# Spectra of a long convolution: one 1024-wide product, sums in PSUM, 64-row halves, and an order written out as a table

## The chip, the cores and the metric

The kernel runs on one core of a Trainium2 chip. The metric is device time in microseconds (us), the median of three runs. A core has five engines that run side by side, each with its own queue in program order: TensorE for matmuls (PE in the profile; PEld is its weight load), VectorE (DVE), ScalarE (ACT), GpSimd (POOL) and SyncE (SP), which here issues the DMAs. Matmuls write to PSUM, in banks of 512 fp32 values for each of 128 partitions. Everything else lies in SBUF.

## The reference

```python
mod = (_silu(c) @ w_mod).reshape(c.shape[0], 6, 1, -1)
h = _layernorm(x, axis=-1) * (1 + ca) + sa
x = x + ga * _A_ref(h, ...)          # the convolution
h = _layernorm(x, axis=-1) * (1 + cb) + sb
x = x + gb * _B_ref(h, ...)          # gated FFN: (silu(h@w1) * (h@w3)) @ w2
...
# in _A_ref: u is h, of length L = 2048 and 640 channels
P = jnp.exp((A * dt[:, None])[:, :, None] * pos[None, None, :])
K = 2.0 * jnp.einsum("dn,dnl->dl", C, P).real
Kf = jnp.fft.rfft(K, L2)             # L2 = 2 * L
Uf = jnp.fft.rfft(u_t, L2)
y = jnp.fft.irfft(Uf * Kf[None, :, :], L2)[:, :, :L]
```

For each of 640 channels a filter `K` of 2048 taps is made from 128 complex modes, the input is convolved with it through Fourier transforms, and the result goes through a layer norm and a gated FFN of width 1728.

## The kernel before

The channels go in five blocks of 128 (b = 0 to 4). For each block four kinds of work run:

- The filter is made in eight chunks of 16 channels (tasks `g`). POOL adds phases (`ph`, 1024 wide) and multiplies magnitudes (`yy`, `xx`, 512 wide, three for each chunk); ACT takes sines (`tr`, in PSUM); DVE multiplies (five instructions on `yy` and `xx`); PE forms the product `kps` in 32 matmuls of 64 columns, four abreast in 32-column groups; ACT copies it to `ks` and DVE adds the skip term (`ks<-kps,dsk`). `yy`, `xx` and `ph` have two buffers each.
- The input is normalised (tasks `h`: ACT or DVE makes `hn`, DVE makes `hb`), goes through a scratch tensor in DRAM and comes back turned (`xb`).
- A first stage of the transform turns `xb` and `ks` each into `sp` (or `sp2` for `xb` of odd blocks), in eight tasks (names `hh` and `k`): eight matmuls into one bank `ps`, then one copy by ACT or DVE.
- The spectra (tasks `w`, eight for each block): PE makes the second stage of both sides, `fh` and `fk`, in PSUM; ACT copies `fh` to `hz`; DVE multiplies the two complex spectra into `fp`. After each second one (tasks `z`, four for each block) PE takes the inverse of `fp` into two banks `fz`, ACT or DVE copies them to `zt`, and SP stores them to the DRAM scratch `zd`.

The complex product before takes four DVE instructions: with r for the real or imaginary half of the input's spectrum, two of 512 values, the second in place in the PSUM bank `fk`, and two of 256 values that take the difference and the sum:

```python
to = k if r else prod[i // 2][:, :, i % 2 * 2:i % 2 * 2 + 2, :].rearrange("p r q d -> p q r d")
nc.vector.tensor_mul(to, k, bc(held[i][:, :, r], 2, 2))
...
k = bank.pop((1, i))
for r, op in enumerate((ALU.subtract, ALU.add)):
    p = prod[i // 2][:, r, i % 2 * 2:i % 2 * 2 + 2, :]
    nc.vector.tensor_tensor(p, p, k[:, :, 1 - r], op=op)
```

When the last block's `zd` is stored, the memory is laid out anew ("border"), the inverse is finished (`iy`, `iyb`), the second layer norm runs, and the FFN follows: matmuls of 512 columns with each operand split into a high and a low part (`fp32r`), PE after PE, to the end. An fp32 matmul has two records in the profile, so a task of eight matmuls is x16 there.

All work up to the first groups of the FFN is entered as tasks in a class `Plan`: name, engine or choice of engines, an estimated duration, what it follows, and which ring buffers it takes and gives back. A ring of four PSUM banks (`bank`) serves `ps`, `fh`, `fk`, `fz`. `Plan.place` plays the tasks through by their estimated durations with a table of ranks (`RANKS`) as priorities, and this sets each engine's order and the choice of engine before anything runs. Each engine then follows that order strictly. All those instructions carry one line number (L157, the recording helper), so they are told apart by tile names.

## Time and profile before

| | us |
|---|---|
| runs: median of 3 (lowest, highest) | 974.97 (973.5, 975.03) |
| profiled execution, its time | 972.31 |
| profiled execution, span from first to last instruction | 970.5 |
| busy in the span: PE, DVE, ACT, POOL | 859.9, 702.0, 546.4, 340.5 |
| last filter product (`kps`) starts, in the span | 346.1 |
| last inverse (`fz`) starts | 374.6 |

A row of a group reads: line, engine, operation, output<-inputs, sizes (partitions x values), count | busy us, mean ns of one | idle time of the engine just before them, and what ended it. A row of the timeline reads: start, duration, engine, line, operation, and in brackets the idle time before it. Instructions of one engine overlap a little at their ends, so the distance from start to start is what one of them takes of the engine.

### The profile page before, as it was taken

How to read it: one execution, taken by the hardware profiler on the slowest of the kernel's cores; microseconds unless marked ns; L12 is line 12 of the kernel's file. 1: busy time of each engine (PE TensorE's matmuls, PEld its weight loads, DVE VectorE, ACT ScalarE, POOL GpSimd, SP SyncE). 2: the span in 40 equal slices, each digit the busy share in tenths (PEclk: the TensorE clock that was granted, in tenths of full speed). 3: DMA queues.
4: the chain of work that ended last, by engine and by line, in shares of the span. 5: the costliest groups of instructions: out<-in, count | busy, mean ns of one | idle time of the engine just before them, and what ended most of it. 6: DMA issues, size and time to landing. Idle time of an engine off the chain costs nothing.

```text
span 970.5 us, 20551 instructions
## 1 busy us (share of the span) xinstructions
PE 859.9 (89%) x7985; PEld 681.8 (70%) x7985; DVE 702.0 (72%) x1395; ACT 546.4 (56%) x1022; POOL 340.5 (35%) x371
## 2 busy tenths in 40 slices
PE   1464787889899997899999999999999999999997
PEld 1132665767778884677777778888788888888775
DVE  7998899999999968886767677557456464645422
ACT  6877788979888851564434455346444344443412
POOL 1797889879799600002111111000011212120000
PEclk9996999999999999799999999999999999999999
DMA  9955453723425268935434422276342322220374
GB/s 218 275 168 191 111 136 95 177 66 106 111 80 152 74 159 206 241 118 182 122 120 139 122 96 68 82 209 194 112 134 64 102 77 86 82 82 28 108 220 133
DMA packets 110506, 127.31 MB, mean 131 GB/s; under 512 B 10568, under 2 KB 90696, under 8 KB 109128
## 3 DMA queue, kind: packets, MB, share of 16 engines
q1 hardware_dynamic: 109032, 125.21, 45.3%
q8 instruction: 63, 1.03, 0.5%
q10 hardware_dynamic: 1376, 0.79, 0.3%
q14 instruction: 35, 0.29, 0.1%
HBM read 95.82 MB, written 30.15 MB: 130 GB/s over the span
## 4 chain that ended last, share of the span: by engine, by line
PE 70%; DVE 17%; ACT 5%; issue 4%; DMA 3%; POOL 1%; SPq 1%; ACTq 0%; DVEq 0%
PE c L157 19%; PE acc L157 18%; PE X L157 12%; PE ps L157 4%; PE gu L157 3%; DVE yy L157 3%; PE kps L157 3%; PE fz L157 2%; PE fk L157 2%; DVE fp L157 2%; PE fh L157 2%; DVE hn L157 2%; DVE xx L157 2%; DVE xb L157 1%; ACT tr L157 1%
## 5 line engine op out<-in xcount | busy, mean ns | idle before, releaser
L157 PE MATMUL acc<-ah,w 128*128 128x512 f32 x560 | 173.2, 395 | 2.4 <-DMA w<-w2d 1.7
L157 PEld LDWEIGHTS acc<-ah,w 128*128 128x128 f32 x560 | 103.7, 188 | 26.4 <-issue 2.1
L157 PE MATMUL acc<-al,w 128*128 128x512 f32 x260 | 102.4, 394 | 0.0
L665 DVE TENSOR_TENSOR wl<-s,wh 128x256 fp32r<-128x256 f32 x92 | 38.9, 423 | 67.5 <-ACT wh L664 67.1
L841 POOL TENSOR_TENSOR s<-wr 128x256 f32<-128x256 f32 x22 | 16.4, 744 | 187.8 <-DMA wr<-in_w 94.8
L157 POOL TENSOR_TENSOR ph<-p,p 128x1024 int32<-128x1024 int32 x40 | 79.2, 1979 | 8.2 <-ACT tr L157 8.0
L664 ACT ACTIVATE wh<-s 128x256 fp32r<-128x256 f32 x92 | 37.6, 410 | 78.5 <-PE X L157 58.1
L157 PE MATMUL kps<-yy,xx 128*32 128x64 f32 x2560 | 51.8, 234 | 28.6 <-DVE xx L157 21.4
L157 DVE TENSOR_TENSOR yy<-yy,tr 128x512 f32<-128x512 f32 (+1 forms) x80 | 75.3, 943 | 1.2 <-ACT tr L157 0.6
L157 PEld LDWEIGHTS kps<-yy,xx 128*32 128x32 f32 x2560 | 45.1, 116 | 38.3 <-issue 22.0
L664 ACT ACTIVATE wh<-wr 128x256 fp32r<-128x256 f32 x92 | 38.4, 418 | 56.0 <-PE X L157 42.3
L842 POOL TENSOR_TENSOR s<-s,wr 128x256 f32<-128x256 f32 x22 | 16.6, 755 | 134.0 <-issue 133.9
L902 ACT ACTIVATE t<-g 128x512 f32<-128x512 f32 x44 | 27.8, 632 | 52.7 <-DVE g L866 52.7
L157 ACT ACTIVATE tr<-ph,hpi 128x512 f32<-128x512 f32 x80 | 54.6, 690 | 4.4 <-DVE xx L157 2.7
L157 PEld LDWEIGHTS acc<-al,w 128*128 128x128 f32 x260 | 48.9, 188 | 10.8 <-DVE al L665 0.3
L871 DVE SCALAR_TENSOR_TENSOR g<-t,g 128x512 f32<-128x512 f32 x48 | 33.7, 702 | 31.3 <-ACT t L902 29.3
L157 POOL TENSOR_TENSOR yy<-e,e 128x512 f32<-128x512 f32 x48 | 52.4, 1109 | 8.8 <-PE kps L157 5.9
L157 DVE TENSOR_TENSOR xx<-tr,xx 128x512 f32<-128x512 f32 x80 | 54.3, 680 | 1.1 <-ACT tr L157 1.1
L157 PE MATMUL ps<-wk,ks 128*64 128x128 f32 x640 | 42.4, 285 | 13.6 <-DVE ks L157 8.9
L157 ACT ACTIVATE tr<-ph 128x512 f32<-128x512 int32 x80 | 47.3, 598 | 12.4 <-DVE yy L157 6.5
L157 PE MATMUL ps<-wk,xb 128*64 128x128 f32 x640 | 46.1, 295 | 6.3 <-ACT sp L157 3.0
L157 PEld LDWEIGHTS ps<-wk,ks 128*64 128x64 f32 x640 | 37.0, 143 | 20.3 <-ACT hn L157 6.6
(448 smaller groups left out, 2379.7 us busy)
## 6 DMA issues: line engine op xcount, KB each, us to landing
w<-w2d SPq DMA_DIRECT2D x42, 640.0 KB, 3.9
wr<-in_w SPq DMA_DIRECT2D x50, 320.0 KB, 3.9
zd<-zt SPq DMA_DIRECT2D x40, 256.0 KB, 2.9
w2d<-w SPq DMA_DIRECT2D x14, 640.0 KB, 3.5
xs<-in_x SPq DMA_DIRECT2D x16, 320.0 KB, 11.3
hs<-hb SPq DMA_DIRECT2D x20, 256.0 KB, 2.5
xb<-hs SPq DMA_DIRECT2D x20, 256.0 KB, 4.9
iz<-zd SPq DMA_DIRECT2D x32, 160.0 KB, 5.0
```

What stands on the lines that cost most here:

```text
L157: self.prev = self.k.order(f(*a, **kw), self.prev)
L664: self.nc.scalar.activation(H, v, AF.Copy)
L665: eng.tensor_tensor(Lo, v, H.bitcast(F32), op=ALU.subtract)
L841: eng.tensor_tensor(s[0], u[:, 0:2], u[:, 2:4], op=ALU.add)
L842: eng.tensor_tensor(s[1], s[0], g[:, 0:2], op=ALU.subtract)
L871: V.scalar_tensor_tensor(g, th, 1.0, g, op0=ALU.add, op1=ALU.mult)
L902: tanh = lambda o, i: A.activation(o, i, AF.Tanh, scale=0.5)
```

## The change

The 1024-wide product: DVE multiplies all four combinations of the halves of `fk` and `hz` in one instruction into a `fp` of twice the size. For blocks 0 to 3 nothing adds them; the inverse has four terms instead of two, with a third set of constants (`wz` grows from two to three), so the sums are made in PSUM. Block 4 keeps two terms and the two 256-wide instructions, now with both operands in SBUF.

The first stage: one task now covers what two did, in 32 matmuls of 64 rows and 64 columns, alternating between the upper and lower 64 rows, into two banks with a copy each. For block 0 most of them take banks from the four-bank ring, after the memory of the start is closed (`inv`).

The exponents of the filter's magnitudes (`al8`) are multiplied into the place that the last exponential then overwrites. Two of the buffers that the inverse loads at the end (`iz`) lie in `sp2`, and their loads follow `inv` rather than the later `change`. The order is a list of task numbers, with a mark where the second choice of engine is taken; nothing is played through any more, and the durations in the task entries have no effect.

The count of DVE instructions goes from 1395 to 1289. Beside the products this comes from the choice of engine: DVE makes 39 of the 80 copies of `ps` (20 before), 13 of the 40 of `fz` (9), and 20 of the 64 instructions that write `hn` from `xq` (44); ACT takes the rest. POOL multiplies two of five `al8` (three before) and one more magnitude (`mag`).

Three places in the order. First DVE, the products of spectra 4 and 5 of block 2 (`fk24`, `fk25`, into `fp24`), among the filter's chunks 464 and 480 (`yy_464` and so on), before:

```order
L157 TENSOR_TENSOR fp24_3590<-fp24_3590,fk24_3566 128x256 x2
L157 TENSOR_TENSOR yy_464_3514<-yy_464_3514,tr0_464_3560 128x16x32
L157 TENSOR_TENSOR xx_464_3513<-tr1_464_3564,xx_464_3513 128x512
L157 TENSOR_TENSOR yy_464_3514<-yy_464_3514,tr3_464_3625 128x1024
L157 TENSOR_TENSOR fp24_3590<-fk25_3648,hz25_3630 128x2x2x128
L157 TENSOR_TENSOR ks3_3326<-kps_383,dsk_85 128x4
L157 TENSOR_TENSOR fk25_3648<-fk25_3648,hz25_3630 128x512
L157 TENSOR_TENSOR xx_464_3513<-tr4_464_3678,xx_464_3513 128x512
L157 TENSOR_TENSOR fp24_3590<-fp24_3590,fk25_3648 128x256 x2
```

and after:

```order
L149 TENSOR_TENSOR fp24_4050<-fk24_3990,hz24_4031 128x4x256
L149 TENSOR_TENSOR yy_464_3877<-yy_464_3877,tr0_464_4033 128x16x32
L149 TENSOR_TENSOR xx_464_3876<-tr1_464_4035,xx_464_3876 128x512
L149 TENSOR_TENSOR yy_464_3877<-yy_464_3877,tr3_464_4055 128x1024
L149 TENSOR_TENSOR ks3_3694<-kps_387,dsk_85 128x4
L149 TENSOR_TENSOR xx_464_3876<-tr4_464_4057,xx_464_3876 128x512
L149 TENSOR_TENSOR ks3_3694<-kps_387,dsk_85 128x4
L149 TENSOR_TENSOR fp24_4050<-fk25_4073,hz25_3914 128x4x256
L149 COPY zt231_4165<-fz231_4040 128x512
```

One instruction stands where four stood; the filter's instructions between them are the same.

Second PE, the first inverse of block 1 (`fz100` and `fz101` are its two banks, `wz` the constants), before:

```order
L157 MATMUL kps_383<-yy_304_2302,xx_304_2301 32x64 x32
L157 MATMUL fz100_2647<-fp10_2380,wz_84 128x512
L157 MATMUL fz101_2648<-fp10_2380,wz_84 128x512
L157 MATMUL fz100_2647<-fp10_2380,wz_84 128x512
L157 MATMUL fz101_2648<-fp10_2380,wz_84 128x512
L157 MATMUL fh14_2662<-sp2_1037,wb_86 64x128 x8
```

and after:

```order
L149 MATMUL fz100_2793<-fp10_2700,wz_84 128x512
L149 MATMUL fz101_2794<-fp10_2700,wz_84 128x512
L149 MATMUL fz100_2793<-fp10_2700,wz_84 128x512
L149 MATMUL fz101_2794<-fp10_2700,wz_84 128x512
L149 MATMUL fz100_2793<-fp10_2700,wz_84 128x512
L149 MATMUL fz101_2794<-fp10_2700,wz_84 128x512
L149 MATMUL fz100_2793<-fp10_2700,wz_84 128x512
L149 MATMUL fz101_2794<-fp10_2700,wz_84 128x512
L149 MATMUL fh14_2803<-sp2_965,wb_86 64x128 x8
```

Four matmuls became eight, and what stands behind them on PE is four matmuls later.

Third PE after the last filter product of all (chunk 624), where the first stage of block 4's filter ends and its spectra begin, before:

```order
L157 MATMUL kps_383<-yy_624_4582,xx_624_4581 32x64 x32
L157 MATMUL ps411_4841<-wk_83,ks4_4131 64x4x16x2 x8
L157 MATMUL ps415_4878<-wk_83,ks4_4131 64x4x16x2 x8
L157 MATMUL ps417_4892<-wk_83,ks4_4131 64x4x16x2 x8
L157 MATMUL ps416_4912<-wk_83,ks4_4131 64x4x16x2 x8
L157 MATMUL fh40_4926<-sp_87,wb_86 64x128 x8
L157 MATMUL fk40_4937<-sp_87,wb_86 64x128 x8
```

After, the 32 rows of `ps4100` and `ps4101` alternate, and then those of `ps4130` and `ps4131`; their last ones and what follows them:

```order
L149 MATMUL ps4131_5473<-wk_83,ks4_4796 64x2x16x2
L149 MATMUL ps4130_5472<-wk_83,ks4_4796 64x2x16x2
L149 MATMUL ps4131_5473<-wk_83,ks4_4796 64x2x16x2
L149 MATMUL fh40_5506<-sp_87,wb_86 64x128 x8
L149 MATMUL fk40_5519<-sp_87,wb_86 64x128 x8
L149 MATMUL fh41_5540<-sp_87,wb_86 64x128 x8
L149 MATMUL fk41_5549<-sp_87,wb_86 64x128 x8
```

Four tasks of one bank became two tasks of two banks; the spectra behind them stand as before. The diff, cut to its core:

```diff
-EXPS = ((0, 0, 0, 64.0), (0, 1, 0, 1.0), (1, 0, 0, 512.0), (1, 1, 4, 8.0), (1, 2, 0, 8.0))
+EXPS = ((0, 0, 0, 64.0), (1, 0, 0, 512.0), (1, 1, 4, 8.0), (1, 2, 0, 8.0), (0, 1, 0, 1.0))
...
-RANKS = """
--1152 -1540 -1534 -1515 -1509 -1417 -1345 -1436 -1412 -1402 -1385 -1330 -1273 -1351 -1452 -1478 -1480 -1475 -1459 -1510 -1507
...
+ORDER = """
+1 80 79 78 81 2 19 20 82 83 41 42 14 21 22 150' 84 151 23 24 15 25 16 3 43 17 44 18 26 4 5 12 6 30 28 45 46 29 47 27 33 7 31 91 48
...
-    wz = np.tile(np.stack([np.block([c, s]), np.block([-s, c])], 1), (2, 1, 1))
+    wz = np.tile(np.stack([np.block([c, s]), np.block([-s, c]), np.block([-c, -s])], 1), (2, 1, 1))
...
-    def place(self, rank):
...
+    def sequence(self):
+        names, uses = list(T), {}
...
+        taken, done, out = {r: [] for r in self.n}, set(), []
+        for x in ORDER.split():
+            n = names[int(x.rstrip("'"))]
+            engs, _, _, after, _, _, take, give, _, _ = T[n]
+            assert n not in done and done.issuperset(after), n
+            for r, y, _ in take:
...
+            out.append((engs[x.endswith("'")], n))
...
-        self.order = self.place({n: t[4] for n, t in T.items()} | dict(zip(searched, found)))
-        for s, f, e, n in self.order:
-            if T[n][2]:
-                T[n][2](e)
+        for e, n in self.sequence():
+            if self.tasks[n][2]:
+                self.tasks[n][2](e)
...
-            if u < 3:
-                z[u] = [self.ip.tile([P, 2, 512], F32, name=f"iz{u}{pr}", tag=f"iz{pr}", bufs=3) for pr in range(2)]
-            else:
-                z[u] = [self.xb[:, 1024 * pr:1024 * pr + 1024].rearrange("p (a d) -> p a d", a=2) for pr in range(2)]
+            s = self.sp2.rearrange("p a b c -> p (a b c)")
+            t = s[:, :2048] if u == 0 else s[:, 2048:] if u == 1 else self.xb if u == 3 else self.ip.tile([P, 2048], F32, name="iz2")
+            z[u] = [t[:, 1024 * pr:1024 * pr + 1024].rearrange("p (a d) -> p a d", a=2) for pr in range(2)]
...
-        plan.add("inv", None, 0, inv, ["cols", "mag1"], 0)
+        plan.add("inv", None, 0, inv, ["cols", "mag1", "hscalef", "colsf", "q0.v1", "q1.v1"] + [f"h0.{i}.a" for i in range(4)] + [f"k0.{i}.e{h}" for i in range(2) for h in range(2)] +
+                 [f"rw{g}" for g in range(4)], 0)
...
         def mm(i):
-            pk[i] = self.psg.tile([P, 512], F32, name=f"ps{b}{m}{i}", tag="f", bufs=3) if b == 0 else self.pbank(f"ps{b}{m}{i}")
-            for e in range(4):
-                x = self.ks[b][:, 4 * i + e, :] if m else xb[:, :, 4 * i + e]
+            for h in range(2):
+                n = f"ps{b}{m}{i}{h}"
+                pk[i, h] = self.psg.tile([P, 512], F32, name=n, tag="f", bufs=3) if early(i) else self.pbank(n)
+            for e in range(8):
+                x = self.ks[b][:, 8 * i + e, :] if m else xb[:, :, 8 * i + e]
                 for r in range(2):
-                    o = pk[i][r * 64:(r + 1) * 64].rearrange("p (v j i f) -> p i j v f", j=4, i=4, f=2)[:, e]
-                    nc.tensor.matmul(o, x, self.wk[:, r, :], start=True, stop=True, tile_position=(0, 64 * r))
-
-        def out(i, e):
-            o = self.spectrum(b, m).rearrange("p v (j i) f -> p v j (i f)", j=4)[:, :, :, 8 * i:8 * i + 8]
-            v = pk.pop(i).rearrange("p (v j x) -> p v j x", v=16, j=4)
+                    for h in range(2):
+                        g = slice(64 * h, 64 * h + 64)
+                        o = pk[i, h][r * 64:(r + 1) * 64].rearrange("p (v j i f) -> p i j v f", j=2, i=8, f=2)[:, e]
+                        nc.tensor.matmul(o, x[g], self.wk[g, r, g], start=True, stop=True, tile_position=(64 * h, 64 * r))
+
+        def out(i, h, e):
+            o = self.spectrum(b, m).rearrange("p v (j i) f -> p v j (i f)", j=4)[:, :, 2 * h:2 * h + 2, 16 * i:16 * i + 16]
+            v = pk.pop((i, h)).rearrange("p (v j x) -> p v j x", v=16, j=2)
             if e == "DVE":
                 nc.vector.tensor_copy(o, v)
             else:
                 nc.scalar.activation(o, v, AF.Copy)
         g = ("hh", "k")[m]
-        bank = "f2" if b == 0 else "bank"
-        for i in range(8):
-            t = W[g](b, i)
+        early = lambda i: b == 0 and m and i < 2
+        for i in range(4):
+            bank = "f2" if early(i) else "bank"
+            t = W[g](b, 2 * i + 1)
             n = f"{g}{b}.{i}."
-            after = [f"g{b}.{i}.d"] if m else [f"h{b}.f"]
+            after = [f"g{b}.{2 * i}.d", f"g{b}.{2 * i + 1}.d"] if m else [f"h{b}.f"]
             if b == 0:
-                after = after + ["wk"]
-            old = ["inv"] if (b, m) == (1, 0) else [f"w{b - 2}.7.f"] if m == 0 and b else [f"w{b - 1}.7.k"] if b else \
+                after = after + ["wk"] + ([] if early(i) else ["inv"])
+            old = ["inv"] if (b, m) == (1, 0) else [f"w{b - 2}.{x}.f" for x in range(8)] if m == 0 and b else [f"w{b - 1}.{x}.k" for x in range(8)] if b else \
                 [f"mr{i}" for i in range(4)] + ([] if m else [f"h0.{i}.a" for i in range(4)])
-            add(n + "m", "PE", 1.04, lambda i=i: mm(i), after + old, t, take=[(bank, 1)])
-            add(n + "e", ("ACT", "DVE"), (.48, .61), lambda e, i=i: out(i, e), [n + "m"], t - W["quick"], give=[(bank, n + "m")])
+            add(n + "m", "PE", 1.1, lambda i=i: mm(i), after + old, t, take=[(bank, 1), (bank, 1, "'")])
+            for h in range(2):
+                add(n + f"e{h}", ("ACT", "DVE"), (.48, .61), lambda e, i=i, h=h: out(i, h, e), [n + "m"], t - W["quick"], give=[(bank, n + "m" + "'" * h)])
...
-        four = lambda x: x.rearrange("p (q r d) -> p q r d", q=2, r=2)
+        last = b == NB - 1
...
-        def product(i, r):
-
-            if i % 2 == 0 and r == 0:
-                prod[i // 2] = self.fpool.tile([P, 2, 4, P], F32, name=f"fp{b}{i}", tag="fp", bufs=FP)
-            k = bank[1, i]
-            to = k if r else prod[i // 2][:, :, i % 2 * 2:i % 2 * 2 + 2, :].rearrange("p r q d -> p q r d")
-            nc.vector.tensor_mul(to, k, bc(held[i][:, :, r], 2, 2))
+        def product(i):
+
+            if i % 2 == 0:
+                prod[i // 2] = self.fpool.tile([P, 2, 2, 4, P], F32, name=f"fp{b}{i}", tag="fp", bufs=FP)
+            k = bank.pop((1, i)).rearrange("p q r d -> p r (q d)")
+            h = held[i].rearrange("p q r d -> p r (q d)")
+            to = prod[i // 2][:, :, :, i % 2 * 2:i % 2 * 2 + 2, :].rearrange("p s r q d -> p s r (q d)")
+            nc.vector.tensor_mul(to, bc(k, 1, 2), bc(h, 2, 2))
 
         def both(i):
 
-            k = bank.pop((1, i))
+            p = prod[i // 2][:, :, :, i % 2 * 2:i % 2 * 2 + 2]
             for r, op in enumerate((ALU.subtract, ALU.add)):
-                p = prod[i // 2][:, r, i % 2 * 2:i % 2 * 2 + 2, :]
-                nc.vector.tensor_tensor(p, p, k[:, :, 1 - r], op=op)
+                nc.vector.tensor_tensor(p[:, 0, r], p[:, 0, r], p[:, 1, 1 - r], op=op)
 
         def inverse(j):
-            p = prod.pop(j).rearrange("p r q d -> p r (q d)")
+            terms = ((0, 0, 0), (0, 1, 1), (1, 1, 2), (1, 0, 1))[:2 if last else 4]
+            p = prod.pop(j).rearrange("p s r q d -> p s r (q d)")
             for f in range(2):
                 bank["z", j, f] = self.pbank(f"fz{b}{j}{f}")
-            for r in range(2):
+            for n, (s, r, w) in enumerate(terms):
                 for f in range(2):
                     g = slice(64 * f, 64 * f + 64)
-                    nc.tensor.matmul(bank["z", j, f], self.wz[g, r, :], p[g, r], start=(r == 0), stop=(r == 1), tile_position=(64 * f, 0))
+                    nc.tensor.matmul(bank["z", j, f], self.wz[g, w, :], p[g, s, r], start=(n == 0), stop=(n == len(terms) - 1), tile_position=(64 * f, 0))
...
-            add(n + "x0", "DVE", .61, lambda i=i: product(i, 0), [n + "k", n + "h"] + ([f"w{b}.{i - 1}.x0"] if i % 2 else []), t - q, take=[] if i % 2 else [("fp", 1)])
-            add(n + "x1", "DVE", .61, lambda i=i: product(i, 1), [n + "x0"], t - q, give=[("hz", n + "h")])
-            add(n + "c", "DVE", .67, lambda i=i: both(i), [n + "x1"], t - q, give=[("bank", n + "k")])
+            add(n + "k", "PE", .92, lambda i=i: of(1, i), firstk + room + [n + "f"], t + .1, take=[("bank", 1)])
+            add(n + "x", "DVE", 1.13, lambda i=i: product(i), [n + "k", n + "h"] + ([f"w{b}.{i - 1}.x"] if i % 2 else []), t - q, take=[] if i % 2 else [("fp", 1)],
+                give=[("hz", n + "h"), ("bank", n + "k")])
+            if last:
+                add(n + "c", "DVE", .67, lambda i=i: both(i), [n + "x"], t - q)
...
-            add(n + "z", "PE", 1.95, lambda j=j: inverse(j), [f"w{b}.{i - 1}.c", f"w{b}.{i}.c"], t + W["late"], take=[("bank", 1), ("bank", 1, "'")],
-                give=[("fp", f"w{b}.{i - 1}.x0")])
+            add(n + "z", "PE", 1.75 if last else 3.45, lambda j=j: inverse(j), [f"w{b}.{i - 1}.{y}", f"w{b}.{i}.{y}"], t + W["late"], take=[("bank", 1), ("bank", 1, "'")],
+                give=[("fp", f"w{b}.{i - 1}.x")])
...
-            if b == 0:
-                x[0] = self.ks[0].rearrange("p e b -> p (e b)")[:, :1024]
-            else:
-                x[0] = self.xsp.tile([P, 4 * D], F32, name="xs_al8", tag="xs", bufs=4)[:, :1024] if b == 1 else self.fpool.tile([P, 1024], F32, name=f"al8{b}", tag="al8", bufs=1)
-            x[0] = x[0].rearrange("p (d j) -> p d j", j=8)
+            x[0] = E[0][:, :, 1, :]
```

202 lines of the change are left out of this document (80 added, 122 removed), and 88 rows, old and new, of tables (ORDER, RANKS).

## The prediction

> **What bounds the kernel now.** I read the busy times by stage first, because the page's 89% for PE is a mean over two very different parts.
>
> ```profile
> core 0: us, PE busy (x) PEld busy (x) DVE busy (x) ACT busy (x) POOL busy (x), PEclk, DMA share, GB/s
> 34.00:100.00 66.00, 35.21 (x608) 20.49 (x608) 60.99 (x102) 51.07 (x93) 59.89 (x56) 0.84 0.62 196
> 100.00:220.00 120.00, 95.50 (x1884) 79.70 (x1886) 114.44 (x219) 99.08 (x168) 103.10 (x103) 0.94 0.46 116
> 220.00:346.00 126.00, 119.35 (x2525) 100.26 (x2526) 117.37 (x213) 104.85 (x181) 104.55 (x101) 1.00 0.39 104
> 346.00:376.00 30.00, 28.83 (x386) 22.10 (x377) 23.23 (x51) 11.50 (x24) 0.00 (x0) 1.00 0.81 205
> 398.00:970.00 572.00, 560.78 (x2501) 446.96 (x2499) 339.73 (x668) 249.38 (x498) 65.82 (x88) 1.00 0.39 120
> ```
>
> From 398 on PE is busy for 560.8 of 572 us: that is the FFN, which the change does not touch. So only the first 398 us can move. From 34 to 346, while filters are made, DVE is busy for 61.0 + 114.4 + 117.4 = 292.8 of 312 us, 94%. But it is not alone: in 220 to 346 PE is busy for 119.4 of 126, and POOL works for 267.5 of the 302 us between these two instructions, its first chunk and its last:
>
> ```profile
> 34.62 2.28 POOL L157 TENSOR_TENSOR ph<-p,p 128x1024 int32<-128x1024 int32 x1
> ...
> 335.43 1.07 POOL L157 TENSOR_TENSOR yy<-e,e 128x512 f32<-128x512 f32 x1
> ```
>
> The waits tell who holds whom. POOL's waits in 40 to 330, then those of PE in 100 to 346 that matter here:
>
> ```profile
> POOL yy L157 <- PE kps L157: 14.9, 11, 3.9
> POOL ph L157 <- ACT tr L157: 8.0, 6, 3.0
> POOL p L157 <- DVE p L157: 2.5, 1, 2.5
> ```
>
> ```profile
> PE kps L157 <- DVE xx L157: 6.9, 7, 2.4
> PE ps L157 <- ACT sp L157: 3.0, 3, 1.5
> PE ps L157 <- DVE sp L157: 2.4, 2, 1.6
> ```
>
> POOL waits for buffers that `kps` frees, `kps` waits for DVE's last product `xx`; ACT keeps `ph` because DVE holds the `tr` banks. So DVE is the head of the queue, with POOL and PE less than a tenth behind. The median of the runs, 974.97, is 2.66 above the profiled 972.31; I sum on 972.31 and add 2.7.
>
> **The products on DVE (removed).** Groups by shape, then start times near the end of blocks 3 and 4:
>
> ```profile
> L157 DVE TENSOR_TENSOR yy<-yy,tr 128x1024 f32<-128x1024 f32 x40 | 48.4, 1210 | 0.9 <-ACT tr L157 0.6
> L157 DVE TENSOR_TENSOR fp<-fp,fk 128x256 f32<-128x256 f32 x80 | 29.7, 411 | 0.2
> L157 DVE TENSOR_TENSOR fk<-fk,hz 128x512 f32<-128x512 f32 x40 | 27.6, 691 | 0.0
> L157 DVE TENSOR_TENSOR fp<-fk,hz 128x512 f32<-128x512 f32 x40 | 27.3, 683 | 3.8 <-PE fk L157 2.7 <-ACT hz L157 0.8
> L157 DVE TENSOR_SCALAR hn<-xq,rs_y_h,rs_n_h 128x128 f32<-128x128 f32 x44 | 18.1, 412 | 1.2
> L157 DVE COPY sp<-ps 128x512 f32<-128x512 f32 x20 | 13.4, 683 | 3.2 <-PE ps L157 3.1
> L157 DVE COPY zt<-fz 128x512 f32<-128x512 f32 x9 | 6.2, 685 | 2.2 <-PE fz L157 2.1
> L157 DVE TENSOR_TENSOR xs_al<-al,j 128x1024 f32<-128x1024 f32 x1 | 2.8, 2835 | 0.0
> L157 DVE TENSOR_TENSOR late<-late,mag 128x512 f32<-128x512 f32 x1 | 1.7, 1718 | 0.0
> ```
>
> ```profile
> 340.66 1.21 DVE L157 TENSOR_TENSOR yy<-yy,tr 128x1024 f32<-128x1024 f32 x1
> 341.79 0.68 DVE L157 TENSOR_TENSOR xx<-tr,xx 128x512 f32<-128x512 f32 x1
> ...
> 351.99 0.69 DVE L157 TENSOR_TENSOR fp<-fk,hz 128x512 f32<-128x512 f32 x1 [1.62 <-PE fk L157]
> 352.60 0.69 DVE L157 TENSOR_TENSOR fk<-fk,hz 128x512 f32<-128x512 f32 x1
> 353.32 0.75 DVE L157 TENSOR_TENSOR fp<-fp,fk 128x256 f32<-128x256 f32 x2
> 353.99 0.68 DVE L157 TENSOR_TENSOR fp<-fk,hz 128x512 f32<-128x512 f32 x1
> ```
>
> One spectrum takes 353.99 - 351.99 = 2.00 us of DVE. The new operation has no row. Its lower end is the 1024-wide `yy<-yy,tr`, with one operand in PSUM and one in SBUF as here: 341.79 - 340.66 = 1.13. Its upper end is the 1024-wide `xs_al`, 2.84, which reads both from SBUF while POOL works. I take 1.13, since the 512-wide product on these very operands (683 ns) lies beside its 1210 in proportion. In blocks 0 to 3 that frees 32 x 0.87 = 27.8 us. Block 4's two sums stay; its 8 x 0.2 lie behind the last chunk, where PE is the bound, and count for nothing.
>
> **Work that changes engine.** From start to start a 512-wide copy takes 0.61 (as 351.99 to 352.60). DVE gets 19 more copies of `ps` (+11.6) and 4 of `fz` (+2.4), loses 24 of `hn` at 0.41 (-9.9) and the `mag` (-1.7). It makes three `al8` for two: at 1.13 to 2.84 each that is -0.7 to +4.5, I take +2. DVE in all: -27.8 + 11.6 + 2.4 - 9.9 - 1.7 + 2 = -23. ACT gives up 19 + 4 copies and takes 24 `hn`; at 255 busy of 312 it has room. POOL multiplies two `al8` for three and one more `mag`: about -1.
>
> **PE: the inverse and the halves.** Start times on PE:
>
> ```profile
> 326.11 1.99 PE L157 MATMUL fz<-fp,wz 64*128 64x512 f32 x8
> 328.03 1.13 PE L157 MATMUL fk<-sp,wb 128*64 128x128 f32 x16
> 329.00 3.14 PE L157 MATMUL ps<-wk,xb 128*64 128x128 f32 x48
> 332.06 1.17 PE L157 MATMUL kps<-yy,xx 128*32 128x64 f32 x64
> ...
> 345.22 1.17 PE L157 MATMUL kps<-yy,xx 128*32 128x64 f32 x64
> 346.32 3.71 PE L157 MATMUL ps<-wk,ks 128*64 128x128 f32 x64
> 349.87 1.08 PE L157 MATMUL fh<-sp,wb 128*64 128x128 f32 x16
> ```
>
> An inverse of two terms takes 328.03 - 326.11 = 1.92; two more terms, 16 times: +30.7. A first-stage task takes 3.06/3 = 1.02 on `xb` and 3.55/4 = 0.89 on `ks`, so two make 1.91. The new task has 64 records of half the columns on a quarter of the array. If all four quarters run abreast, half of 1.91: 0.95. If only two do, 1.91. The nearest row is `kps`: 64 records of 64 columns, four abreast, 346.32 - 345.22 = 1.10. I take 1.10: 40 x (1.10 - 1.91) = -32.4. PE in all: -2, its load unchanged.
>
> The Trainium skill speaks against this (TensorE: Matmul & The Clock Gate, "Wait — 56ns, not 53.3ns?"): the distance between matmul starts never falls below about 25 ns, however few the columns. By that the task would take 64 x 25 = 1.6 us and PE's load would grow by 40 x (1.6 - 1.91) + 30.7 = 18 where I have -2. The trace disagrees for `kps`, with 1.10 us / 64 = 17 ns; whether it does for quarters of the array, no row here shows.
>
> **What of DVE's 23 us arrives.** Each other engine sets a limit. POOL's listed waits are 25.4 us, and without any of them it would end 25 earlier; some remain, since `yy` and `ph` have only two buffers. If three quarters go (they all lead back to DVE), that is 19. PE in 100 to 346 is busy for 95.5 + 119.4 = 214.9 of 246 us; at the density it already reaches in 220 to 346 (119.35/126 = 0.947) it would need 213/0.947 = 225, so 21 less. I take POOL's 19. Behind the last chunk two new tasks replace four: 2.2 for 3.55, with `fh` starting straight after, -1.4. Then all goes as before: spectra, the last inverse, its store, the border.
>
> The third set of `wz` constants is half as much again of one load at the start, long before the first inverse: nothing. The earlier loads of `iz` ease DMA in 346 to 376 (share 0.81), but PE is busy there for 28.8 of 30 us and so waits for none of them: nothing. The buffers `fp` stay two, and each is held 1.9 longer by the inverse; `kps` and `fh` behind it come that much later, which is one reason why not all of POOL's waits go.
>
> Sum: 972.3 - 19 - 1.4 = 951.9, and 2.7 for the median: 954.6, rounded 955.
>
> **The rivals.**
>
> *All of it arrives* (20%). POOL loses all 25.4, and some of the 9 us that it idles beyond its listed waits (302 - 267.5 - 25.4). For it: nearly all of POOL's waits lead to DVE. Against it: DVE, PE and POOL would each be some 95% busy at once, each in strict order. 942 to 950.
>
> *Banks take the gain* (16%). The halves are made twice as fast, two banks at a time of four, but the copies (0.6 us each, on ACT and DVE) are no faster. Before, PE waited 3.0 + 2.4 us for such copies. If each of some 36 tasks up to 346 waits 0.35 longer, half a copy, PE's limit of 21 shrinks by 13: 975 - 8 - 1 = 966, with a spread of 962 to 972.
>
> *PE becomes the bound* (12%), the one on the other side. If quarters run two abreast, a task costs 1.91, PE gains 30.7 and saves nothing: 214.9 + 30.7 = 245.6, which at 0.947 takes 259 us for 246. That is +13: 988. It decides from where PE's load fills its 246 us at that density, 233: 18 above now, so 30.7 + 36 x (X - 1.91) = 18 and X = 1.56 us a task. Against it: `kps` at 1.10 with as many records.
>
> *A floor under the starts* (4%). If the quarters do run abreast but their 64 records start more slowly than those of `kps`, the task lies between 1.10 and 1.91; about the middle, at 1.5 to 1.6, PE's load just fills its time and nothing is gained: 973 to 977. Against it the same row. The rule of the Trainium skill quoted above is such a floor (TensorE: Matmul & The Clock Gate, the section named there); by its 1.6 us the load would be 214.9 + 30.7 - 11 = 234.6, the stretch 1.7 longer, the time 977.
>
> **How the numbers follow.** My forecast (a gain of 13 to 24, so 951 to 962) has 48%, the full gain 20, the banks 16, PE the bound 12, the floor 4. A difference of 0.2%, 2 us, is about what a measurement of this kernel can tell from no change. Faster: 48 + 20 + 16 = 84. Within: 4. Slower: 12. The range is 940 to 972: it holds the first three cases and leaves out the last two.
>
> **What the profile of the changed kernel would show.** The product: 40 rows `fp<-fk,hz` 128x1024 near 1.2 us; a mean near 2 would end the DVE term. The halves: runs of 64 `ps` records some 1.1 us from start to start; from 1.56 PE would have no wait left in 100 to 346 and the last `kps` would come after 346. The rest: last `kps` near 327; POOL's waits for `kps` and `tr` near 6 instead of 23; DVE busy less than 94% before it; from the last `kps` to the end the 624 us of before (970.5 - 346) less one or two. Waits of `ps` for `sp` well above 5 would mean the banks. I am wrong if the FFN's part moves, or if the start, whose order changes too, comes out later than the gain is large.

## The result, and the profile after

The changed kernel takes 1008.28 us (median of 4 runs, 1005.15 to 1009.53) beside 975.0 for the kernel before: a ratio of 1.0339, with a 95% interval of 1.0312 to 1.0367. It is 33 us slower. The forecast of 955, its range of 940 to 972 and its sign were wrong.

The same stretches of the changed kernel's profile (span 1007.7), the last two moved by 40 us so that they hold its last filters and the spectra behind them:

```profile
core 0: us, PE busy (x) PEld busy (x) DVE busy (x) ACT busy (x) POOL busy (x), PEclk, DMA share, GB/s
34.00:100.00 66.00, 31.58 (x552) 17.42 (x552) 56.37 (x102) 46.64 (x87) 52.29 (x50) 0.79 0.62 200
100.00:220.00 120.00, 87.11 (x2128) 71.91 (x2128) 95.17 (x157) 96.73 (x170) 91.75 (x93) 0.80 0.42 116
220.00:346.00 126.00, 116.27 (x2763) 91.12 (x2765) 95.95 (x137) 85.40 (x142) 96.60 (x95) 0.96 0.30 77
346.00:386.00 40.00, 37.07 (x967) 29.51 (x966) 29.70 (x45) 28.14 (x50) 25.40 (x22) 1.00 0.43 117
386.00:416.00 30.00, 27.61 (x420) 20.05 (x412) 21.26 (x37) 11.32 (x24) 0.00 (x0) 1.00 0.75 193
```

DVE did become free: 96.0 of 126 us where it had 117.4. But POOL is less busy in each of the first three stretches, so chunks are made more slowly, and PE in 220 to 346 is nearly as busy as it was (116.3 for 119.4) while it serves fewer of them. The waits of POOL in 40 to 370 say who keeps it:

```profile
POOL yy L149 <- PE kps L149: 28.5, 14, 5.1
POOL ph L149 <- ACT tr L149: 19.7, 10, 4.0
POOL xx L149 <- PE kps L149: 12.0, 5, 6.3
```

POOL waits 60 us where I had forecast 6. The groups by shape of DVE, PE and PE's weight loads:

```profile
L149 DVE TENSOR_TENSOR fp<-fk,hz 128x1024 f32<-128x1024 f32 x40 | 48.5, 1219 | 13.1 <-PE fk L149 13.1
...
L149 DVE TENSOR_TENSOR fp<-fp 128x256 f32<-128x256 f32 x16 | 6.0, 420 | 0.2
...
L149 PE MATMUL ps<-wk,xb 64*64 64x64 f32 x1280 | 46.1, 294 | 8.7 <-DVE hb L149 3.9 <-ACT zt L149 2.2 <-ACT sp L149 1.3
...
L149 PE MATMUL ps<-wk,ks 64*64 64x64 f32 x1280 | 28.3, 239 | 8.5 <-DVE ks L149 3.6 <-issue 3.0 <-ACT sp L149 1.4
...
L149 PEld LDWEIGHTS ps<-wk,xb 64*64 64x64 f32 x1280 | 43.4, 217 | 12.4 <-ACT tr L149 3.3 <-ACT zt L149 2.6 <-issue 2.4
...
L149 PEld LDWEIGHTS ps<-wk,ks 64*64 64x64 f32 x1280 | 25.1, 152 | 13.3 <-issue 4.6 <-ACT tr L149 3.8 <-ACT sp L149 1.6
```

The product is what I said (1219 ns for 1210 of `yy`). The halves have two prices: on `ks` PE is busy for 28.3 us (42.4 before), on `xb` for 46.1, to the tenth what the 128-row tasks took. Start times on PE show the same:

```profile
251.11 7.14 PE L149 MATMUL fz<-fp,wz 64*128 64x512 f32 x32
258.18 2.24 PE L149 MATMUL ps<-wk,xb 64*64 64x64 f32 x64
260.35 1.17 PE L149 MATMUL kps<-yy,xx 128*32 128x64 f32 x64
261.44 1.16 PE L149 MATMUL ps<-wk,ks 64*64 64x64 f32 x64
262.43 2.21 PE L149 MATMUL ps<-wk,xb 64*64 64x64 f32 x64
264.42 1.42 PE L149 MATMUL ps<-wk,ks 64*64 64x64 f32 x64
```

A pair of `xb` costs 260.35 - 258.18 = 2.17 (2.04 as two old tasks), a pair of `ks` 0.99 (1.78), an inverse 3.54 (1.92). PE's load grows by 16 x 1.62 + 20 x (2.17 - 2.04) - 20 x (1.78 - 0.99) = 13 us, where I had -2. The chain that ends last, in 220 to 360, of the kernel before and then of the changed one:

```profile
by line: PE ps L157 16.7%; PE fz L157 12.7%; PE fk L157 12.0%; PE fh L157 11.2%; PE kps L157 10.3%; issue 6.0%; ACT tr L157 5.3%; DVE yy L157 4.9%; DVE fp L157 3.7%; DVE xx L157 2.9%; DVE sp L157 2.6%; ACT sp L157 2.6%; ACT ph L157 2.5%; DV
```

```profile
by line: PE fz L149 25.9%; PE ps L149 16.5%; PE kps L149 14.5%; PE fh L149 14.1%; PE fk L149 12.6%; issue 4.7%; DMA hs<-hb 3.2%; ACT tr L149 1.9%; DVE fp L149 1.7%; ACT sp L149 1.2%; POOL yy L149 1.1%; DVE sp L149 0.9%; POOL p L149 0.9%; AC
```

PE's five kinds of matmul carry 63% of it before and 84% after. But the loss does not begin there. When POOL starts the n-th chunk (`ph`), by the timeline:

| chunk | before | after | later by |
|---|---|---|---|
| 10 | 103.3 | 116.0 | 12.7 |
| 19 | 177.0 | 197.7 | 20.7 |
| 31 | 272.9 | 301.7 | 28.8 |
| 40 | 329.9 | 368.9 | 39.0 |

A third is lost by 116, before the first four-term inverse has run (143). From the last `kps` (384.53) to the end it is 623.2 us, 625.3 before: there the forecast held.

### The profile page after: what moved, and what is told of

Same layout as the page of the kernel before. It is cut to its first block, busy times and chain, and to the rows that moved or that the text cites. A ratio compares the mean times of both kernels' runs of the same rounds, so it can differ in the third digit from the quotient of the medians.

```text
span 1007.7 us, 23257 instructions
## 1 busy us (share of the span) xinstructions
PE 877.5 (87%) x9393; PEld 688.7 (68%) x9393; DVE 686.3 (68%) x1289; ACT 545.8 (54%) x1023; POOL 340.3 (34%) x372
## 4 chain that ended last, share of the span: by engine, by line
PE 72%; DVE 10%; DMA 7%; ACT 6%; issue 4%; SPq 1%; POOL 0%; ACTq 0%; DVEq 0%
PE c L149 18%; PE acc L149 17%; PE X L149 11%; PE fz L149 5%; PE ps L149 5%; PE gu L149 3%; PE kps L149 3%; DMA xs<-in_x 3%; PE fh L149 3%; PE fk L149 3%; ACT tr L149 2%; DVE yy L149 2%; DVE fp L149 1%; DVE hn L149 1%; DMA hs<-hb 1%
## 5 line engine op out<-in xcount | busy, mean ns | idle before, releaser
L149 PE MATMUL kps<-yy,xx 128*32 128x64 f32 x2560 | 55.2, 245 | 43.0 <-DVE ks L149 21.6
L149 PEld LDWEIGHTS kps<-yy,xx 128*32 128x32 f32 x2560 | 48.2, 123 | 52.8 <-issue 27.0
L149 DVE TENSOR_TENSOR yy<-yy,tr 128x512 f32<-128x512 f32 x80 | 75.7, 947 | 9.4 <-ACT tr L149 9.1
L149 PE MATMUL fz<-fp,wz 64*128 64x512 f32 x288 | 69.6, 612 | 0.2 <-DVE fp L149 0.2
L586 ACT ACTIVATE wh<-wr 128x256 fp32r<-128x256 f32 x92 | 38.3, 418 | 55.8 <-PE X L149 42.4
L149 DVE TENSOR_TENSOR fp<-fk,hz 128x1024 f32<-128x1024 f32 x40 | 48.5, 1219 | 13.1 <-PE fk L149 13.1
L149 PE MATMUL ps<-wk,xb 64*64 64x64 f32 x1280 | 46.1, 294 | 8.7 <-DVE hb L149 3.9
L149 PEld LDWEIGHTS ps<-wk,xb 64*64 64x64 f32 x1280 | 43.4, 217 | 12.4 <-ACT tr L149 3.3
```

The source lines that it names most:

```text
L149: self.prev = self.k.order(f(*a, **kw), self.prev)
L586: self.nc.scalar.activation(H, v, AF.Copy)
```

## The experiments

Two theories stood first. *Order* (A): the new table makes the engines wait. *Work* (B): PE has too much to do. Each run was made beside the kernel before on the same chip (972.5 to 974.8). The diffs of the runs give the edits in outline, shortened; each run's name stands in its heading.

**The old ranks with the new work (e1).**

```diff
-        for e, n in self.sequence():           # the table
+        self.order = self.place(ranks)         # planner and ranks of the kernel before
```

> The changed kernel's work, task for task, but its table of positions is taken out: the planner and the ranks of the kernel before set the order and the engines (a pair's rank is the lower one of its two old tasks, a product has the rank of the first of its two old multiplications). Theory A, the order: the changed kernel loses 15 us before its first four-term inverse has run (its 27th `yy<-yy,tr` group is that much late at 100 to 130), where PE is far from full, so the table is what costs; then this kernel comes to 960 to 985 and its 40th `ph` starts before 345. Theory B, the work: PE has some 15 us more to do (inverse +27 by 3.63 for 1.92, halves on `ks` -14, halves on `xb` nothing), and any order is late by it; then this kernel stays at 998 to 1012.

As it ran, a pair had the rank of the old task of its own number, 0 to 3, which is somewhat earlier than said. 1004.4, ratio 1.0315 (1.0247 to 1.0382). The early loss is gone: the 60th of the 120 products `yy<-yy,tr`, three to a chunk, starts at 203.2, before the 207.6 of the kernel before. Then it falls behind at once, the 66th at 237.1 for 217.6, in this stretch:

```profile
200.00:250.00 50.00, 50.00 (x1208) 41.39 (x1208) 31.44 (x45) 29.87 (x52) 25.37 (x26) 1.00 0.25 68
```

PE has no moment free in it. So the table loses the start, and the work, under another order, loses nearly as much in one piece when PE is full. The time is what theory B expected.

**The work undone under the new table**, in parts (e2, e3 and e4, in this order).

```diff
-            nc.tensor.matmul(o, x[g], self.wk[g, r, g], ...)     # halves
+            nc.tensor.matmul(o, x, self.wk[:, r, :], ...)        # 128 rows: e2, e4
-            terms = (...)[:2 if last else 4]
+            terms = (...)[:2]; both(i) behind each product       # e2, e3
```

> The changed kernel with its table of positions as it is, but the work on PE as before: first stages by 128 rows into the same two banks, two-term inverses in all blocks, and behind each 1024-wide product the two 256-wide sums on DVE within the same task. PE has 27 us less for the inverses and 14 more for the first stages, DVE 32 x 0.8 = 26 more. Theory A, the order: the start is as late as in the changed kernel (15 us at 110), and nothing is won back: 1000 to 1015. Theory B, the work: 975 to 988, since the work is that of the kernel before.

> The changed kernel with two-term inverses in blocks 0 to 3 as well, and the two 256-wide sums on DVE within the product's task; halves and table as they are. PE has 16 x 1.7 = 27 us less, DVE 26 more. Theory A, the order: the table leaves DVE 20% idle, so DVE's sums fit into its waits and PE's relief is not used either: 995 to 1008. Theory B, the work on PE: most of PE's 27 comes off: 980 to 990.

> The changed kernel with the first stages by 128 rows, a pair of old tasks in the place of each new one and into the same two banks; inverse, products and table as they are. What the halves are worth: by the starts in the changed kernel's profile a pair on `ks` costs 1.09 by halves (1.78 before) and a pair on `xb` 2.05 to 2.2 (2.04 before). Theory A, the order: 1005 to 1012, since PE is not what holds it. Theory B, the work: 14 us more on PE, of which those up to the last `kps` count: 1013 to 1022.

1029.3, 1040.1 and 999.6. The first two fell to neither theory: the sums, which here read both operands from SBUF, cost more than they did when one lay in PSUM (411 ns before), as the group in the first of them shows:

```profile
L149 DVE TENSOR_TENSOR fp<-fp 128x256 f32<-128x256 f32 x80 | 57.8, 763 | 1.3
```

763 is a mean of two kinds: the 64 sums of blocks 0 to 3 take 849 ns, twice the price of before, and the 16 of block 4, behind the last chunk, where POOL does nothing, take 420, as they do in the changed kernel. So DVE got 54 us and not 26, and these two runs say nothing of the order. The third is the surprise: with some 13 us more for PE the kernel is 8.6 us faster. Halves cost.

**The old order as a table, and the parts of the work in it (o1 to o4, in this order).** Order and engines are what the planner gave the kernel before, task by task. The old product here is two 512-wide multiplications and sums that read PSUM, in one task.

```diff
 ORDER = """
-1 80 79 78 81 2 19 20 82 83 41 ...
+(the old order by names, pairs where their second task stood)
```

> A table again, but with the order and the engines that the planner gave the kernel before, task by task by name (a pair of first-stage tasks stands where its second one stood, a product where its first multiplication stood; what is not free there yet comes a few places later). The work is undone: first stages by 128 rows, products as two 512-wide multiplications with two sums that read one operand in PSUM, two-term inverses. What is left of the change: first-stage tasks in pairs that take two banks at once, the product's parts in one piece, `al8` in place, the loads into the new places. Theory A (the order) and theory B (the work) both expect the time before, 972 to 985; far above it would mean a third thing, the pairs or the new places.

> The same old order and engines, with the 1024-wide products and the four-term inverses of the changed kernel, first stages by 128 rows. PE has 27 us more than in the old work, DVE 28 less. Theory A (the order): no slower than the one with the old work, 965 to 985, since PE still has waits. Theory B (the work): PE's 119 us of 126 in 220 to 346 leave no room, so most of the share of the 27 that falls behind 190 comes through: 990 to 1003.

> The same old order and engines, with the old products and two-term inverses and the first stages by 64-row halves. PE has some 14 us less (halves on `ks`), DVE the same. If halves help as predicted: 2 to 8 us under the one with the old work. If they cost, as in the run of the changed kernel with 128 rows (8.6 us): 5 to 10 us above it.

> The same old order and engines with all of the changed kernel's work. Theory A: 970 to 990, and the start as in the kernel before (27th `yy<-yy,tr` group within 5 us). Theory B: 995 to 1010, late from 190 on where the inverses come thick.

999.8, 1005.8, 1029.0, 1031.1. Theory A falls as the whole explanation: with all the new work this old order (o4) is 23 us worse than the new table (1031 for 1008). It loses less at the start, the 10th chunk 0.9 late and the 19th 5.7, where the table has 12.7 and 20.7, and more behind it. What in the table costs the start was not looked for. Nor does the table gain anything as such: o4's order was made for other work, and the planner's order for the new work (e1, 1004.4) is no slower than the table. Halves cost 29 and 25, the new inverse 6 and 2. And o1 is 27 us above the kernel before with the same work, which called for a third theory (C): the pair, which takes two banks at once.

**Single tasks again (s1 and s2).** As o1 and o2, with the first stage in eight tasks of one bank per group.

```diff
-        for i in range(4):
-            add(n + "m", "PE", 1.1, ..., take=[(bank, 1), (bank, 1, "'")])
+        for i in range(8):
+            add(n + "m", "PE", 1.04, ..., take=[(bank, 1)])
```

> The old order and engines as in the earlier runs of them, and the old work (128-row first stages, two 512-wide multiplications with sums that read PSUM, two-term inverses); but the first stage in single tasks of one bank each, eight to a group, as in the kernel before. What is left of the change is `al8` in place and the loads into other places. Theory C, formed on those runs (999.8 with pairs, 1029 with pairs in halves, under the old order): a pair that takes two banks and gives both to the copies only behind its last record is what costs, 25 us. By C this kernel comes to 972 to 980. If the new places cost, it stays near 995.

> Single first-stage tasks of 128 rows and the old order and engines, with the 1024-wide products and four-term inverses of the changed kernel: that part of the change alone. Theory C with PE's load at the bound (the work theory): PE has 27 us more, DVE 28 less; 980 to 995. If DVE was the bound and PE has room, as predicted: 955 to 968.

984.0 and 991.8, ratios 1.0129 (1.0088 to 1.017) and 1.019 (1.0153 to 1.0227). Under one order, then, single tasks take 984, pairs of 128 rows 1000, pairs in halves 1029. What ACT and DVE wait for in 100 to 350 follows, for the three in that order:

```profile
ACT sp L151 <- PE ps L151: 7.7, 13, 1.5
```

```profile
ACT sp L149 <- PE ps L149: 20.2, 17, 2.7
...
DVE sp L149 <- PE ps L149: 5.4, 6, 1.5
```

```profile
ACT sp L149 <- PE ps L149: 36.8, 19, 7.4
...
DVE sp L149 <- PE ps L149: 17.7, 7, 6.2
```

Copies of `ps` wait 8, 26 and 54 us (DVE's have no such wait in the first run). Over their whole spans the changed kernel's copies wait 29 us for `ps`, those of the kernel before 13. A single task can be copied while the next one runs; of a pair of 128 rows the first bank is full half way; of a pair in halves both are full only at its end, and in strict order everything behind those copies waits with them. The growth of these waits (18 and 29 us) is near that of the time (16 and 29). That is theory C as far as these runs carry it: I varied the tasks, not that wait alone, and from pairs of 128 rows to halves other things change too. In the chain of 220 to 360 the time in which an engine waits for nothing that the profile shows ("issue") grows from 13 to 21 us (9.3 and 14.9%), and PE's granted clock in 220 to 346 falls from 0.95 to 0.87. So the cause of the 29 is in part argued. The last 11 us of s1 over the kernel before (`al8` in place, the loads into other places, the product's parts in one piece) were not separated.

**Why halves on `xb` are slow, and the banks one by one (c1 and c2).**

```diff
-                x = ... if m else xb[:, :, 8 * i + e]                     # 64 columns, 32 apart
+                x = ... if m else self.xb[:, 64 * (8 * i + e):][:, :64]   # c1: 64 neighbours
-            for e in range(8): for r in range(2): for h in range(2):
+            for h in range(2): for e in range(8): for r in range(2):      # c2
```

> The changed kernel, but the first stages on `xb` read 64 neighbouring columns for their weights instead of 64 columns that lie 32 apart; it computes another thing there (the input's part of the convolution is wrong) with the same number and shape of instructions, in the same order. If it is the stride that keeps a weight load at 217 ns and 64 records at 2.05 to 2.2 us, they fall to the 1.09 of those on `ks`, PE is rid of some 20 us, and the time falls by 5 to 20 us. If it is something else of `xb`, both stay.

> The changed kernel with the records of a halved task in another order: all of the first bank, then all of the second, so that the first copy can begin half way; the halves of the rows then no longer alternate. Theory C: the copies come earlier, and if the two halves of the columns abreast are as fast as four quarters (1.1 us), it falls by 3 to 8 us; if two abreast take 1.8 to 2.2 us for 64 records, PE has up to 14 us more on `ks`, and it comes to 1000 to 1015.

1011.5 and 1049.5. The stride is the cause: with neighbouring columns PE's time on `xb` falls from 46.1 to

```profile
L149 PE MATMUL ps<-wk,xb 64*64 64x64 f32 x1280 | 26.6, 226 | 12.4 <-DVE hb L149 4.5 <-ACT zt L149 2.3 <-DVE sp L149 2.0
...
L149 PEld LDWEIGHTS ps<-wk,xb 64*64 64x64 f32 x1280 | 23.3, 140 | 16.8 <-issue 3.9 <-ACT tr L149 3.3 <-ACT zt L149 2.7
```

Yet 20 us off PE gained nothing. The chain of that run tells where they went: in 220 to 360 "issue" has 19.1% of it, 26.7 us, where the changed kernel has 4.7%, 6.6 us. A piece of it:

```profile
262.87 2.18 PE ps L149 x128
265.05 1.54 issue
266.59 2.22 PE ps L149 x128
268.81 1.24 issue
270.05 0.93 PE ps L149 x49
270.98 1.06 PE fh L149 x16
272.04 1.07 PE kps L149 x59
273.11 4.01 issue
```

In this piece PE pauses after every 124 to 128 records. In c2 the quarters no longer alternate and PE's time grows, to 73.2 us on `xb` and 52.2 on `ks`; 51 us more for PE cost 41. So what an earlier first copy is worth could not be seen there, and stays open.

**The supply of instructions (m1), the load on PE (p1), and the inverse in the kernel before (b1 to b4).** Theory D: 128 records with their weight loads are one block of PE's instructions, and blocks come at a limited rate.

```diff
+# m1: nothing but matmuls of the first stage's two shapes
+rows("rn", 256, 1); quarters("qn", 128, 1); quarters("qs", 64, 32); rows("rs", 128, 32); quarters("qf", 64, 4)
-            terms = (...)[:2 if last else 4]
+            terms = (...)[:2]                                    # p1, half of each product left out
-                # kernel before: two multiplications, two sums, two terms
+                # b1: one 1024-wide, four terms, b < 4;  b2: b < 2
```

> No convolution at all: five long runs of matmuls of the first stage's two shapes on one engine, nothing to wait for but each other (the output is a copy of the input). rn: 128 rows, weights from 64 neighbouring columns, 1024 records; qn: quarters of 64 rows, neighbouring columns, 1024 records; qs: quarters, columns 32 apart, 512 records; rs: 128 rows, columns 32 apart, 512 records; qf: quarters, columns 4 apart, 512 records. Theory D, the supply of instructions: qn starts 128 records at 17 ns and then pauses, and keeps no better mean than 25 to 32 ns, 26 to 33 us in all; rn, at 28 ns, hardly pauses. Without such a limit qn takes 1024 x 17 ns = 17.4 us. The stride: qs and rs at 32 ns each; qf tells from which stride.

> The changed kernel with only the first two of four terms in each inverse, and no sums on DVE in their place: half of each complex product is left out, and nothing else. PE has 16 x 1.7 = 27 us less, in 128 records; DVE, ACT, POOL and the order stay. If PE's load is the bound from 220 us on, as its share of the chain there says (78%), 12 to 20 us come off: 988 to 996. If the order alone holds it, 1003 to 1010.

> The kernel before, with its order and engines kept as a table, and one part of the change alone: the 1024-wide product and the four-term inverse in blocks 0 to 3 (for room, `al8` of blocks 2 to 4 lies in a buffer of x that is idle until then, and one of the border's inputs in the second spectrum buffer). The prediction's term: DVE 28 us less, three quarters of POOL's waits gone, 955 to 960. The work theory, from the two runs with single tasks (991.8 against 984.0): DVE's relief arrives up to some 200 us, then PE is the bound and gives it back with some more: 974 to 984.

> The same in blocks 0 and 1 alone, whose inverses run up to some 220 us, where DVE has the fewest waits and PE is busy for 80 to 86%. From the two runs with single tasks, where the one with the new inverse led by 5 us at the 22nd chunk and lost it later: 965 to 971. If it makes no difference where the trade is made: as the run with four blocks.

m1 confirms D. The chain in 75 to 103, while `qn` runs (its 1024 records fill 75.2 to 102.6), has seven pauses; the first two and the last:

```profile
78.65 1.57 issue
...
82.32 1.36 issue
...
100.69 1.36 issue
```

Between pauses 128 records take 2.1 us, 16 ns each; with them the mean is 27.4 / 1024 = 27 ns. In the strided groups there is no pause: their quarters keep 32 and 30 ns a record (`qs`, `qf`), which is slower than those 27. The 128-row groups took 56 and 63 ns a record (`rn`, `rs`), twice what I had expected. The weight loads:

```profile
L42 PEld LDWEIGHTS qna<-wk,xt 64*64 64x64 f32 x512 | 15.6, 135 | 12.0 <-issue 12.0
...
L42 PEld LDWEIGHTS qsa<-wk,xt 64*64 64x64 f32 x256 | 16.2, 220 | 0.1
...
L42 PEld LDWEIGHTS qfa<-wk,xt 64*64 64x64 f32 x256 | 15.4, 213 | 0.1
```

A weight load takes 135 ns from neighbours, 213 from columns 4 apart (16 bytes), 220 from 32 apart. Its 128-row forms take 140 and 219 (`rn`, `rs`): the rows do not matter, so a halved task has twice the loads at the full price each.

p1: 994.6, which is 13.7 under the changed kernel for 27 us less on PE. Its chain in 220 to 360 begins

```profile
by line: PE ps L149 12.9%; ACT tr L149 12.0%; issue 10.1%; PE kps L149 9.0%; PE fh L149 8.8%; DVE yy L149 8.7%; ACT ph L149 6.0%; PE fk L149 5.5%; DVE fp L149 5.1%; DVE xx L149 4.9%; DVE sp L149 2.8%; PE fz L149 2.8%; ACT ks L149 2.0%; ACT 
```

with 39% on PE in place of 84. So PE's load was the bound there, and half of what is taken off comes off the time; behind it the other engines stand close.

b1 and b2: 998.3 and 983.2. Both carry an error of mine. For room I had borrowed a buffer of x, and its loads now stood ahead of the input's fetch on SP's queue. In b2, then in the kernel before:

```profile
247.88 1.25 SPq L153 DMA_DIRECT2D x<-in_x  x2
249.22 1.80 SPq L153 DMA_DIRECT2D xb<-hs  x4
```

```profile
237.99 0.54 SPq L157 DMA_DIRECT2D x<-in_x  x1
241.57 1.76 SPq L157 DMA_DIRECT2D xb<-hs  x4
```

So both were made again with those loads behind the fetch, the second with POOL relieved too.

```diff
-    lx0.0, lx0.1 behind exp4, ahead of h3.f
+    lx0.0, lx0.1, lx0.2 beside lx0.3, behind h3.f                # b3 (b < 4), b4 (b < 2)
-    POOL: three table doublings, al8 and mag of block 2
+    DVE                                                           # b4
```

> The kernel before, its order and engines as a table, with the 1024-wide product and the four-term inverse in blocks 0 to 3 and nothing else of the change; as in the earlier run of this, but the loads of x that use the borrowed buffer stand behind the fetch of the input. If those loads were a false 7.6 us there: 988 to 993. What is left above the time before is then the part's own price: PE's 27 us as far as they fall behind 220, less what DVE's relief brings before. The prediction's 955 to 960 is not expected any more.

> The same in blocks 0 and 1 alone, and POOL relieved in that stretch: the doublings of three phase tables (2.2 us of POOL each), `al8` of block 2 (2.0), `mag` of block 2 (1.1) and two small copies go to DVE, 11 us less for POOL and some 7 more for DVE, which the product has relieved by 14. If POOL is what takes over the chain there, a part of the relief arrives: 966 to 972. If PE or the strict order holds it: 974 to 980.

991.4, ratio 1.0187 (1.0157 to 1.0217), and 987.1, ratio 1.0142 (1.0119 to 1.0165). b3 is the cleanest test of the prediction's main term: the kernel before with the wide product and the four-term inverse alone is 17 us slower, where I had forecast 19 us of gain. Its windows (columns as above), the waits of POOL in 40 to 330, the chain in 100 to 220 of the kernel before and of b3, and b3's in 220 to 360:

```profile
100.00:220.00 120.00, 101.06 (x1928) 81.89 (x1924) 106.37 (x178) 99.08 (x169) 103.17 (x103) 0.96 0.45 113
220.00:346.00 126.00, 117.77 (x2193) 90.95 (x2192) 92.41 (x136) 89.78 (x156) 98.73 (x96) 0.99 0.37 95
```

```profile
POOL yy L153 <- PE kps L153: 13.2, 11, 3.0
POOL ph L153 <- ACT tr L153: 11.8, 8, 3.6
POOL xx L153 <- PE kps L153: 5.2, 5, 2.2
```

```profile
by line: DVE yy L157 13.5%; DVE hn L157 10.8%; issue 10.4%; DVE fp L157 10.2%; PE ps L157 7.5%; DVE xx L157 7.2%; PE kps L157 5.3%; DMA xq<-in_x 4.6%; ACT hn L157 4.2%; DVE fk L157 3.9%; PE fk L157 3.4%; DVE hb L157 3.2%; PE fz L157 2.9%; P
```

```profile
by line: POOL ph L153 9.7%; DVE hn L153 8.8%; PE ps L153 8.6%; POOL yy L153 8.5%; PE fz L153 7.8%; issue 7.5%; PE kps L153 7.4%; DVE yy L153 7.1%; POOL p L153 5.1%; DMA xq<-in_x 4.6%; DVE xx L153 4.3%; ACT tr L153 4.0%; POOL xx L153 2.6%; D
```

```profile
by line: PE fz L153 26.0%; PE ps L153 19.2%; PE kps L153 13.2%; PE fk L153 11.9%; PE fh L153 10.7%; issue 6.0%; DVE yy L153 2.3%; DVE sp L153 2.2%; DVE hn L153 1.7%; POOL ph L153 1.4%; DVE xx L153 1.4%; POOL step L153 0.9%; POOL p L153 0.8%
```

DVE is freed (92.4 for 117.4 in the second stretch) and POOL waits no less for `kps` and `tr`, 30 us where it had 24. Up to 220 the run leads by at most 3.1 us (23rd chunk): in the chain POOL's own rows (26%) have taken much of DVE's place (49% before). From 220 on PE has 81% of the chain, and the lead turns into a lag of 0.4 at the 25th chunk and 18.4 at the 40th. The borrowed buffers do not make that lag: b1 and b2 share them and the order too, and differ in blocks 2 and 3 alone. Both are 8.9 late at the 31st chunk; at the 40th b1 is 23.0 late and b2 9.5. These are prices under an order made for the old work; an order planned for this part alone was not tried, nor blocks 0 and 1 with the loads behind the fetch and nothing else. b4 shows that DVE cannot simply be given POOL's work: its 19th chunk is 7.8 late. No run beats the kernel before, which stays the fastest; the nearest are b2 (983.2) and s1 (984.0).

## Why the prediction was wrong, point by point

- *The bound.* "POOL and PE less than a tenth behind" DVE was read rightly, and its consequence was not drawn: a lead of a few per cent on two other engines leaves a few per cent to gain. "So DVE is the head of the queue" rested on POOL's waits in the kernel before; in b3, with DVE freed, the waits for `kps` and `tr` are 30 us for 24.
- *The product* (1.13 us a spectrum): right, 1219 ns.
- *The halves* (1.10 a pair): right on `ks` (0.99), wrong on `xb` (2.17). The row that I took, `kps`, has neighbouring columns; the strided load of the `xb` tasks stood in the trace of before as a separate group, at 220 ns for 143 on `ks`, and I did not look at weight loads. PE's load came to +13 instead of -2.
- *The inverse* (+1.92 each): +1.62 to 1.71, a little less than said.
- *What arrives* (POOL's 19 us): this is the step that failed. I let DVE's relief through to POOL and set PE's load at -2. By itself the part costs 17 us (b3). Two thirds of PE's 27 us (88 of the 128 `fz` records of blocks 0 to 3, by the kernel before) fall into 220 to 346, where PE is busy for 95% of the time; DVE's 28 come off an engine that then waits. My own rule of density, 0.947, gives 9 us of loss for +27 on PE. For the +13 of the whole change it gives a limit of 5 us of gain and some 968. So the size of the halves is not all that was wrong: their waits and the order, which the sum left out, come on top.
- *The floor and the rule quoted beside it.* The Trainium skill (TensorE: Matmul & The Clock Gate, "Wait — 56ns, not 53.3ns?") has no start below some 25 ns. Single bursts disagree, at 16 ns; the mean over 1024 records, 27 ns, lies near it, but through the pauses that m1 shows. On `ks` the rule was wrong for a pair and on `xb` too kind; its 977 was nearer than my 955, which is luck.
- *The banks.* I priced this rival at a small wait of PE for copies, 0.35 us a task. The wait seen runs the other way: copies wait for the pair. Under the old order pairs cost 16 us and halves 29 more.
- *PE becomes the bound* (988, 12%): the right sign and part of the mechanism; the halves are dear through their strided weight loads, not by running two abreast. A pair costs (0.99 + 2.17) / 2 = 1.58, at the stated point of decision of 1.56. p1 gives 14 of the 33 us back for 27 less on PE; what the pairs cost came on top of it.
- *The order.* I named the start as a way to be wrong, and it is 12.7 us late at the 10th chunk. Against the old order carried over, the table as a whole is 23 us better for this work (1008 for 1031); against the planner's order (e1, 1004) it is not. How much of the 33 each part has can't be given as a sum, since under one order a part costs 29 and under the other 9.
- *The tail* (-1.4): right, -2.1.

## What to carry to other kernels

Where three engines stand within a tenth of each other in strict order, look in each stretch at what would be second before relieving one: here 28 us off DVE, paid for with 27 on PE, lost 17. Before costing a split matmul, look at its weight loads: they do not shrink with the rows, and their columns' stride sets their price. A task that fills two banks should be counted with the wait of those who empty them, not only with its own time; here these waits grew about as the time did, though no run changed them alone.

## What the runs showed of the hardware that was not expected

- PE's instructions come in blocks. After 128 records with their 128 loads, 256 instructions, it pauses for 1.4 to 1.9 us when they run at 16 ns (m1); m1's instruction queue moved 0.46 MB in 28 packets, 16 KB each. The Trainium skill describes such blocks (Runtime: NRT & Kernel Launch, "Instruction fetch mechanics": refills of 16 KiB, 256 instructions) and holds that their fetch is mostly hidden; in m1, at 16 ns a record, it is not.
- Weight loads from columns 16 bytes apart cost nearly as much as from 128 apart (213 and 220 ns, 135 from neighbours). The Trainium skill (SBUF — State Buffer, "Door 1: The DMA port swizzle") tells of lines of 16 bytes, with a penalty for each access that goes to a new one. The trace agrees as far as these three spacings go; none between was run.
- Sums on DVE with both operands in SBUF took 849 ns while POOL worked and 420 while it did not (e2); with one operand in PSUM they take 411 over all blocks of the kernel before and 416 in block 4 alone (b3).
- The clock that PE was granted was lower where PE had less to do: 0.80 in 100 to 220 after, with PE busy for 87 us, and 0.94 before, with 95.5. A `kps` record took 263 ns there for 231. So PE's work gets longer just when it waits, and no run here separates the two.
